# Weight splits gated on the last tiles' copies, and five register reads moved behind two transposes

## The chip, the core and the metric

The kernel runs on one core of one Trainium2 chip. Five engines work side by side: TensorE (PE in the profile, with its weight loads as PEld), VectorE (DVE), ScalarE (ACT), GpSimd (POOL) and SyncE (SP). Each has its own queue, whose instructions start in order; they wait for each other through semaphores. SP computes nothing here: it issues nearly all DMAs. The metric is the device time of one execution in microseconds (us), and of several executions the median.

## The reference

Three layers in a row: an attention with a decay bias, a dense layer with a cosine gate, and a layer of eight experts, each token going to one of them.

```python
def _attn_ref(q, k, v, s):          # 2 batches, 8 heads, 576 rows, 64 wide
    scores = scale * np.matmul(q, k.transpose(0, 1, 3, 2))
    cum = np.cumsum(np.maximum(s, 0.0), axis=-1)
    bias = -(cum[:, :, :, None] - cum[:, :, None, :])
    scores = np.where(causal, -1000000000.0, scores + np.minimum(bias, 0.0))
    attn = softmax(scores)          # written out in the reference
    return np.matmul(attn, v)

def _moe_ref(x, w_in, w_out):       # 1152 tokens, 512 -> 2048 -> 512
    h = x @ w_in
    return (h * np.cos(h)) @ w_out

def _moe2_ref(x, w_gate, w1, w2, capacity):   # 8 experts, 512 -> 1024 -> 512, capacity 288
    logits = x @ w_gate
    expert_idx = np.argmax(logits, axis=1)
    # each token is kept, in order, while its expert has had fewer than capacity tokens
    h = np.maximum(np.einsum('ecd,edf->ecf', disp, w1), 0.0)
    y = np.einsum('ecf,efd->ecd', h, w2)
    out[i] = gate_w[i] * y[expert_idx[i], pos[i]]
```

## The kernel before

The 1152 tokens are nine tiles T of 128. The attention and the first dense product (`l1`) fill the time up to about 200 us. The second dense product (`l2_mm`, line 867) makes the tiles' 512 outputs; `l2_end` copies a tile's result out of PSUM. For the last two tiles (T of 7 and 8, `T >= NDT`) it first makes a float32 copy `xq` (line 856); `route_a` turns that with four PE transposes (line 900) and copies the turned tile back to `xq` (line 902). `route_b` computes the logits and the token's place, and scatters the tile's rows into a buffer in HBM, `disp` (line 947, an indirect DMA issued by POOL), where each expert has a region of 288 rows.

After the scatter of tile 7 the first 144 rows (`HEAD`) of two experts are read from `disp`, turned by a DMA transpose into `eX` (line 1013), and computed while tile 8 is still being routed. After tile 8, `counts` finds on DVE, as integers in the tile `si`, the order of the five experts that have not been chosen yet (`si[0:5]`, line 1192) and the first row that is left of each of the two head experts (`si[8:10]`, line 1200), and in `fl` which of six sizings fits. SP reads these integers into registers, one `values_load` each, and needs them as addresses: the two first rows for the transposes of the remaining rows of the head experts, the five expert numbers for the weights and rows of the other experts.

Then the program branches on `fl`. In the arm, `experts` computes expert after expert: `e_meta` loads scale and token number of each row into `eM` (line 1020), `e_rows` a DMA transpose into `eX`, and `e_weights` streams float32 weights of 512 KB a piece into four staging buffers `ws` (lines 969 and 973). Each piece is split into two float16 halves by `split`: an ACTIVATE on ACT (line 658) and a SCALAR_TENSOR_TENSOR on DVE (line 659). `expert` multiplies with `eX` (line 1044) and the hidden tile `eH` (line 1066), turns the result (1073), scales it by `eM` (1052) and scatters it to the output (1053).

A scheduler sets the order on each engine from dependencies and from hints. A hint is given by `after`: it holds an instruction, in the schedule, behind those that a dictionary `gate` has recorded under some keys.

```python
def after(keys, fn, *args):
    with ExitStack() as es:
        for key in keys.split():
            if key in gate:
                es.enter_context(tc.issue_after(gate[key].ins))
        return fn(*args)
```

Of the kernel before, what the change touches and what calls it, by code (L numbers as in the profile page):

```python
# [14 lines left out]
AF = mybir.ActivationFunctionType  # L15
# [12 lines left out]
NK = 3  # L28
NF = 1
NH = 2  # L30
# [47 lines left out]
def kernel(ctx, tc, q, k, v, s, w_in, w_out, wg, w1, w2, out, cap, wide):  # L78
    nc = tc.nc
# [3 lines left out]
    E, _, F = w1.shape  # L83
# [12 lines left out]
    NS = -(-cap // 32) * 32  # L96
    HEAD = 144
# [47 lines left out]
    cnt = const.tile([128, 1, E], F16, name="cnt")  # L145
# [45 lines left out]
    gate = {}  # L191
# [509 lines left out]
# [6 lines that stand above are left out]
# [145 lines left out]
    def l2_end(T, xp):  # L852
        r = work.tile([128, ROW], I32, tag="row", name="row", bufs=6)
        xf = xq[:, 0:DM] if T >= NDT else None
        if T >= NDT:
            nc.scalar.activation(xf, xp, AF.Copy, scale=2.0 ** -2)
        rh = r[:, 0:DM].bitcast(F16)
        nc.scalar.activation(rh[:, 0:DM], xp, AF.Copy, scale=2.0 ** -8)
        nc.vector.scalar_tensor_tensor(rh[:, DM:2 * DM], xp, 2.0 ** -8, rh[:, 0:DM], ALU.mult, ALU.subtract)
        nc.gpsimd.tensor_copy(r[:, DM + 1:ROW], tokid[:, T:T + 1])  # L860
        rows[T] = (r, xf)
# [29 lines left out]
    def route_a(T):  # L891
        r, xf = rows[T]
        if T < NDT:
            xr = work.tile([128, 2 * KD, 128], F16, tag="xr", name="xr", bufs=2)
            nc.sync.dma_start_transpose(out=xr, in_=r[:, 0:DM].bitcast(F16))
            rows[T] = (r, xr)
        else:
            tp = bank("pt")
            for kk in range(KD):
                nc.tensor.transpose(tp[:, kk * 128:(kk + 1) * 128], xf[:, kk * 128:(kk + 1) * 128], idf)  # L900
            xt = xq[:, DM:2 * DM].rearrange("p (k t) -> p k t", k=KD)
            nc.scalar.copy(xt.rearrange("p k t -> p (k t)"), tp)
            rows[T] = (r, xt)

    def route_b(T):
# [53 lines left out]
    def e_weights(plan, lo=0, hi=None):  # L959
        n = KD + KE // 2  # L960
        items = [(e, src, i) for e, src in plan for i in range(n)][lo:hi]
        pend = []

        def ld(e, src, i):
            t = staging()
            src = src() if callable(src) else src
            if i < KD:
                s1 = w1[e, i * 128:(i + 1) * 128, :] if src is None else w1v[bass.ds(src * DM + i * 128, 128), :]
                nc.sync.dma_start(t, s1)
            else:  # L970
                j = (i - KD) * 256
                s2 = w2[e, j:j + 256, :] if src is None else w2v[bass.ds(src * F + j, 256), :]
                nc.sync.dma_start(t.rearrange("p (a d) -> p a d", a=2), s2.rearrange("(a p) d -> p a d", p=128))
            pend.append(t)

        todo = list(items)

        def fill(n):
            while todo and len(pend) < n and not (callable(todo[0][1]) and todo[0][1]() is None):
                ld(*todo.pop(0))  # L980

        fill(len(ws) - 1)
        yield
        for e, src, i in items:
            fill(len(ws))
            b_ = (win, wb[0:2], wb[2:4], wout)[e % 4]
            a = [b_[0].rearrange("p a b -> p (a b)").rearrange("p (k c f) -> p k c f", k=KD, c=2), b_[1].rearrange("p a b -> p (a b)").rearrange("p (k c f) -> p k c f", k=KE, c=2)]
            ew[e] = a
            t = pend.pop(0)
            if i < KD:  # L990
                after("ev cnt", split, a[0][:, i, 0, :], a[0][:, i, 1, :], t, 64.0)
            else:
                j = (i - KD) * 2
                after("ev cnt", split, a[1][:, j:j + 2, 0, :], a[1][:, j:j + 2, 1, :], t.rearrange("p (a d) -> p a d", a=2), 64.0)
            yield

    ex_ = {}
# [9 lines left out]
    def e_rows(e, ns, rows_):  # L1007
        i = eb["n"]
        eb["n"] += 1
        n16 = -(-ns // 16) * 16  # L1010
        xo = i % XR * 2 * KD * 224 if ns <= 224 else i % 2 * 2 * KD * n16
        X = eb["X"][:, xo:xo + 2 * KD * n16].rearrange("p (k n) -> p k n", k=2 * KD)
        nc.sync.dma_start_transpose(out=X, in_=rows_[0:n16, 0:DM].bitcast(F16))  # L1013
        ex_[e] = (X, i)
# [8 lines left out]
    def at(src, off, ns):  # L1023
        n16 = -(-ns // 16) * 16
        return disp[bass.ds(src * NS if off is None else off, n16), :]
# [63 lines left out]
    def run(*gens):  # L1089
        live = [[g, n, 0.0] for g, n in gens]  # L1090
        while live:
            live.sort(key=lambda z: z[2])
            z = live[0]
            try:
                next(z[0])
                z[2] += 1.0 / z[1]
            except StopIteration:
                live.remove(z)

    def take(gen, n):  # L1100
        for _ in range(n):
            next(gen, None)
            yield

    def seq(*gens):
        for g in gens:
            yield from g
# [36 lines left out]
    SP = (mybir.EngineType.SP,)  # L1144
# [61 lines left out]
            gate["cnt"] = V.tensor_reduce(fl, ky[:, 0:len(LIMITS)], AX.X, ALU.add)  # L1206
        return fl, si

    def registers(fl, si):
        order = [nc.values_load(si[0:1, r:r + 1], engines=SP, min_val=0, max_val=E - 1) for r in range(E - NK)]  # L1210
        first = [nc.values_load(si[0:1, E + h:E + h + 1], engines=SP, min_val=0, max_val=(E - 1) * NS + HEAD) for h in range(NH)]
        return order, first

    def experts(plan, group):
        saved = dict(ew), dict(eb), list(ws), dict(ex_)
        n = len(plan)

        def rows(e):
            src, ns, off = plan[e]
            rows_ = disp[e * NS:(e + 1) * NS, :] if src is None else at(src, off, ns)  # L1220
            if len(ex_.get(e, ())) != 2:
                e_rows(e, ns, rows_)
            e_meta(e, ns, rows_)

        depth = 2 if plan[0][1] <= 224 else 1
        for e in range(depth):
            rows(e)
        have = 0 if plan[0][0] is None else 16 + WP
        feed = e_weights([(e, plan[e][0]) for e in range(n)], have)
        gens = [expert(e, plan[e][1], group) for e in range(n)]  # L1230
        done = [0] * n
        l2s = [KD if flipped(m) else blocks(m)[0] for _, m, _ in plan]
        state = {"fed": have, "credit": -E0 * EF, "finished": 0, "l1": 0}
        next(feed)

        def pull(upto):
            while state["fed"] < min(upto, 8 * n, 8 * (state["finished"] + 4) + HALF * 4 * (state["l1"] > state["finished"])):
                next(feed)
                state["fed"] += 1

        gate.pop("ev", None)
        gate.pop("cnt", None)

        def adv(e, k):
            if e >= n:
                return
            pull(8 * (e + 1))
            while done[e] < k and next(gens[e], "end") != "end":
                done[e] += 1
                ns = plan[e][1]  # L1250
                cols = 512 * blocks(ns)[0] if not flipped(ns) else 2 * ns
                state["credit"] += EF * (12 * ns if done[e] <= KE else 12 * cols) / 2400
                pull(have + int(state["credit"]))

        la, lb = (LA, LA + LB) if depth == 2 else (0, 0)
        for e in range(n):
            if depth == 1 and e + 1 < n:
                rows(e + 1)
            adv(e, KE)
            state["l1"] = e + 1  # L1260
            adv(e + 1, la)
            if depth == 2 and e + 2 < n:
                rows(e + 2)
            adv(e, KE + l2s[e])
            adv(e + 1, lb)
            adv(e, KE + l2s[e] + 1)
            state["finished"] = e + 1
        ew.update(saved[0])
        eb.update(saved[1])
        ws[:] = saved[2]  # L1270
        ex_.clear()
        ex_.update(saved[3])
# [24 lines left out]
    with ExitStack():  # L1297
        if True:
# [35 lines left out]
            regs = counts()  # L1334
            for _ in range(KE // 2):
                next(pre)
            order, first = registers(*regs)
            for h in range(NH):
                n = max(p[h] for p in PROFILES)
                e_rows(h, n, at(P["o"][h], first[h], n))  # L1340
            run((seq(take(phase, KE - RF), take(phase1, LA), phase, phase1), 2 * (KE + KD)), (take(pre, items), W3P))
            level = nc.values_load(regs[0], min_val=0, max_val=len(LIMITS))

# [41 lines left out]
```

## Time and profile before

| | |
|---|---|
| median of three executions | 432.86 us (428.65, 432.86, 433.86) |
| the profiled execution, its own time | 430.29 us |
| its span, first to last instruction | 428.2 us |
| granted TensorE clock, mean of the span | 0.988 |
| busy: PE, DVE, ACT, POOL | 395.1, 311.8, 274.8, 149.2 us |

The span lies inside the time of the profiled execution; 2.1 us are around it. All views below are of that one execution, and their times count from the start of the span. A row of a timeline gives start, duration, engine, line, operation, tiles and, in brackets, how long the engine had been idle before it and what ended that.

### The profile page before, as it was taken

To read this page: it belongs to the slowest core of one execution; us is meant where nothing else is said; L and a number is where in the kernel's file an instruction comes from. 1 tells how busy PE (TensorE), PEld (TensorE's weight loads), DVE (VectorE), ACT (ScalarE), POOL (GpSimd) and SP (SyncE) were. 2 spreads that over 40 slices of the span, in tenths; PEclk is the share of its full clock that TensorE was granted. 3 is DMA by queue.
4 is the path that set the end of the run, shared out by engine and by line. 5 is a ranking of instruction groups with operands and counts; after the bars stand their busy time and mean duration, and the time that the engine had idled before them with its cause. 6 is when DMAs were issued, how large, how long until landed. Compare 5 with 4: busy or idle time off the path is not lost.

```text
span 428.2 us, 10640 instructions
## 1 busy us (share of the span) xinstructions
PE 395.1 (92%) x3928; PEld 281.6 (66%) x3928; DVE 311.8 (73%) x768; ACT 274.8 (64%) x630; POOL 149.2 (35%) x261
## 2 busy tenths in 40 slices
PE   2799999999999999999999999797998999999783
PEld 2588888886666666654444454354997999987552
DVE  7769999749999599989885664672842477877670
ACT  6679989986878677775234532533734477777560
POOL 7668887563554445455000032010011011122100
PEclk9989999999999999999999999899999999999998
DMA  7979795203369932323667456947759298998851
GB/s 166 210 173 190 165 203 151 72 2 100 98 188 328 369 124 92 88 70 98 183 204 230 116 128 206 280 110 222 252 148 216 61 314 264 308 330 265 264 209 30
DMA packets 90003, 77.38 MB, mean 181 GB/s; under 512 B 62768, under 2 KB 70960, under 8 KB 89942
## 3 DMA queue, kind: packets, MB, share of 16 engines
q1 hardware_dynamic: 86934, 71.62, 59.5%
q0 software_dynamic: 1952, 4.73, 3.2%
q8 instruction: 33, 0.54, 0.5%
q10 hardware_dynamic: 1056, 0.26, 0.3%
q14 instruction: 28, 0.23, 0.2%
HBM read 57.66 MB, written 12.28 MB: 163 GB/s over the span
## 4 chain that ended last, share of the span: by engine, by line
PE 32%; DMA 9%; DVE 7%; issue 5%; ACT 4%; SPq 2%; POOL 1%; POOLq 0%; ACTq 0%; DVEq 0%
DMA ws<-in_moe_w_dram 8%; PE ps_mm L867 7%; PE ps_sm L867 5%; PE ps_pt L1044 3%; PE ps_s L1066 3%; PE ps_mm L1044 2%; PE ps_s L867 2%; PE ps_pt L867 2%; PE ps_s L1044 2%; PE ps_pt L1066 2%; PE ps_mm L1066 2%; DVE gall L659 1%; ACT gall L658 1%; DVE y L818 1%; SPq L1013 1%
## 5 line engine op out<-in xcount | busy, mean ns | idle before, releaser
L812 PEld LDWEIGHTS <-win 128*128 128x128 f16 x576 | 56.3, 98 | 37.0
L867 PEld LDWEIGHTS <-gall 128*128 128x128 f16 x432 | 41.3, 98 | 49.3 <-issue 2.5
L867 PE MATMUL ps_mm<-wout,gall 128*128 128x512 f16 x240 | 57.9, 387 | 0.3 <-DVE n__2954 L826 0.3
L659 DVE SCALAR_TENSOR_TENSOR gall<-ws,gall 128x1024 f16<-128x1024 f32 x32 | 38.8, 1221 | 23.2 <-ACT gall L658 22.1
L1053 POOL DMA_INDIRECT out_dram<-gall,eM x15 | 18.8, 1252 | 98.4 <-ACT gall L1052 77.4
L658 ACT ACTIVATE gall<-ws 128x1024 f16<-128x1024 f32 x32 | 33.7, 1056 | 26.8 <-DMA ws<-in_moe_w_dram 26.8
L658 ACT ACTIVATE wout<-ws 128x512 f16<-128x512 f32 (+1 forms) x32 | 27.3, 860 | 23.7 <-DVE ws L681 18.5
L241 ACT ACTIVATE z<-z,st 128x256 f32<-128x256 f32 (+4 forms) x72 | 41.9, 586 | 0.7 <-DVE st L241 0.7
L947 POOL DMA_INDIRECT disp<-row,rsli x9 | 9.2, 1017 | 94.0 <-ACT rm L928 48.5
L241 DVE CUSTOM_DVE_ANT_0 z<-ps_s,zm 128x512 f32<-128x512 f32 (+3 forms) x72 | 34.5, 511 | 10.0 <-PE ps_s L244 8.8
L659 DVE SCALAR_TENSOR_TENSOR wout<-ws,wout 128x512 f16<-128x512 f32 (+1 forms) x32 | 30.4, 955 | 8.2 <-ACT wout L658 8.0
L812 PE MATMUL ps_s<-xT,win 128*128 128x384 f16 x192 | 34.2, 326 | 0.0
L812 PE MATMUL ps_pt<-xT,win 128*128 128x384 f16 x192 | 33.8, 326 | 0.0
L812 PE MATMUL ps_mm<-xT,win 128*128 128x384 f16 x192 | 33.8, 326 | 0.0
L247 PE MATMUL ps_pt<-idf,z 128*128 128x128 f32 x192 | 30.2, 282 | 1.3 <-DVE p L241 1.3
L1044 PEld LDWEIGHTS <-gall 128*128 128x128 f16 x480 | 27.0, 97 | 3.7 <-issue 1.9
L825 ACT ACTIVATE y<-y,quarter 128x384 f32<-128x384 f32 x48 | 29.2, 609 | 0.1
L241 ACT COPY p<-ps_pt 128x512 f32<-128x512 f32 (+2 forms) x48 | 25.2, 525 | 5.9 <-PE ps_pt L247 5.5
L659 DVE SCALAR_TENSOR_TENSOR win<-ws,win 128x1024 f16<-128x1024 f32 x16 | 19.4, 1225 | 11.7 <-ACT win L658 11.7
L247 PEld LDWEIGHTS ps_pt<-idf,z 128*128 128x128 f32 x192 | 23.1, 144 | 6.3 <-issue 1.5
L244 PE MATMUL ps_s<-kT,qT 128*128 128x384 f16 (+7 forms) x128 | 23.9, 307 | 1.1 <-DMA kT<-bt 0.6
L658 ACT ACTIVATE win<-ws 128x1024 f16<-128x1024 f32 x16 | 16.8, 1055 | 10.9 <-DMA ws<-in_moe_w_dram 10.9
(495 smaller groups left out, 891.9 us busy)
## 6 DMA issues: line engine op xcount, KB each, us to landing
ws<-in_moe_w_dram SPq DMA_DIRECT2D x64, 512.0 KB
ws<-in_moe_w_in_dram SPq DMA_DIRECT2D x16, 512.0 KB
ws<-in_moe_w_out_dram SPq DMA_DIRECT2D x16, 512.0 KB
disp<-zc SPq DMA_DIRECT2D x18, 257.0 KB
out_dram<-zc SPq DMA_DIRECT2D x9, 256.0 KB
qf<-in_q_dram SPq DMA_DIRECT2D x16, 128.0 KB
vf<-in_v_dram SPq DMA_DIRECT2D x16, 128.0 KB
kf<-in_k_dram SPq DMA_DIRECT2D x14, 128.0 KB
```

Of the source, the lines that this page charges most:

```text
L241: return pin(f(*a, **kw))
L244: return pin(nc.tensor.matmul(out_, **kw))
L247: return pin(nc.tensor.transpose(out_, in_, id_))
L658: nc.scalar.activation(hi, src, AF.Copy, scale=sc)
L659: (eng or nc.vector).scalar_tensor_tensor(lo, src, sc, hi, ALU.mult, ALU.subtract)
L812: nc.tensor.matmul(hp[:, 0:CH], lhsT=win[a][:, kk, fs], rhs=xT[:, x_, kk, xs], start=(n == 0), stop=(n == 3 * KD - 1))
L825: nc.scalar.activation(y, y, AF.Sin, scale=TWO_PI, bias=quarter)
L867: gate["pe"] = nc.tensor.matmul(xp, lhsT=G[c][:, a, f, ts], rhs=wout[w_][:, f, :], start=(f == 0 and n == 0), stop=(f == KF - 1 and n == 2))
L947: sc = nc.gpsimd.indirect_dma_start(out=disp, out_offset=bass.IndirectOffsetOnAxis(ap=sli.bitcast(U32), axis=0), in_=r, in_offset=None, bo ...
L1044: gate["pe"] = nc.tensor.matmul(hp[:, 0:ns], lhsT=a1[:, kk, a, fs], rhs=X[:, x_ * KD + kk, 0:ns], start=(n == 0), stop=(n == 3 * KD - 1))
L1053: sc = nc.gpsimd.indirect_dma_start(out=out, out_offset=bass.IndirectOffsetOnAxis(ap=M[:, b, 1:2].bitcast(U32), axis=0), in_=y, in_offset= ...
L1066: nc.tensor.matmul(yp[:, 0:ns], lhsT=a2[:, f, w_, d * 128:(d + 1) * 128], rhs=Hh[:, a, f, :], start=(n == 0), stop=(n == 3 * KE - 1))
```

## The change

Two edits. First, the copies of the last two tiles to `xq` are recorded in `gate["xq"]`, and the splits of the experts' weights are hinted behind them, as they were behind `ev` and `cnt` already. Second, the seven register reads on SP are parted: the two first rows are read, then the two transposes of the remaining rows are issued, then the five expert numbers are read.

```diff
@@ l2_end
         if T >= NDT:
-            nc.scalar.activation(xf, xp, AF.Copy, scale=2.0 ** -2)
+            gate["xq"] = nc.scalar.activation(xf, xp, AF.Copy, scale=2.0 ** -2)
@@ route_a
-            nc.scalar.copy(xt.rearrange("p k t -> p (k t)"), tp)
+            gate["xq"] = nc.scalar.copy(xt.rearrange("p k t -> p (k t)"), tp)
@@ e_weights (and the same in its other arm)
-                after("ev cnt", split, a[0][:, i, 0, :], a[0][:, i, 1, :], t, 64.0)
+                after("ev cnt xq", split, a[0][:, i, 0, :], a[0][:, i, 1, :], t, 64.0)
@@
-    def registers(fl, si):
-        order = [nc.values_load(si[0:1, r:r + 1], engines=SP, min_val=0, max_val=E - 1) for r in range(E - NK)]
-        first = [nc.values_load(si[0:1, E + h:E + h + 1], engines=SP, min_val=0, max_val=(E - 1) * NS + HEAD) for h in range(NH)]
-        return order, first
+    def registers(si):
+        return [nc.values_load(si[0:1, E + h:E + h + 1], engines=SP, min_val=0, max_val=(E - 1) * NS + HEAD) for h in range(NH)]
+
+    def others(si):
+        return [nc.values_load(si[0:1, r:r + 1], engines=SP, min_val=0, max_val=E - 1) for r in range(E - NK)]
@@ experts
-        gate.pop("ev", None)
-        gate.pop("cnt", None)
+        for key in ("ev", "cnt", "xq"):
+            gate.pop(key, None)
@@
-            order, first = registers(*regs)
+            first = registers(regs[1])
             for h in range(NH):
                 n = max(p[h] for p in PROFILES)
                 e_rows(h, n, at(P["o"][h], first[h], n))
+            order = others(regs[1])
```

On SP, after the last weights of the head experts, the order before had all seven reads of `si` ahead of the two transposes into `eX`. TENSOR_LOAD is a read, and the ISA rows behind it are register arithmetic; the semaphore in brackets is what the instruction waits for, DMASW0 being that of the scatter of tile 8. Four more pairs of reads like the first stand ahead of this piece.

```order
L1210 TENSOR_LOAD si
L1210 ISA x2
L1211 TENSOR_LOAD si [waits DVE_49]
L1211 ISA x2
L1211 TENSOR_LOAD si
L1211 ISA x2
L1013 ISA
L1013 DMA_TRANSPOSE eX<-disp 128x8x80 [waits DMASW0_49]
L1013 ISA
L1013 DMA_TRANSPOSE eX<-disp 128x8x80
L1342 TENSOR_LOAD fl [waits DVE_49]
```

In the changed kernel the same place on SP begins with the two reads of the first rows (now line 1210), and line 1213 is that of the other experts' numbers.

```order
L1210 TENSOR_LOAD si [waits DVE_49]
L1210 ISA x2
L1210 TENSOR_LOAD si
L1210 ISA x2
L1013 ISA
L1013 DMA_TRANSPOSE eX<-disp 128x8x80 [waits DMASW0_49]
L1013 ISA
L1013 DMA_TRANSPOSE eX<-disp 128x8x80
L1213 TENSOR_LOAD si
L1213 ISA x2
```

Five reads have moved from ahead of the transposes to behind them; four more pairs like the last follow, then the read of `fl`, the branch and the arm's DMAs, which stand as before. The transposes keep their wait.

On ACT, these are the rows around the copies of tile 8 (`xq`, lines 856 and 902) and the weight splits (line 658) in the changed kernel.

```order
L658 ACTIVATE gall<-ws_90 128x1024 [waits DMAHW7_49]
L856 ACTIVATE xq<-ps_mm 128x512 [waits PE_49]
L858 ACTIVATE row<-ps_mm 128x512 [waits DMAHW6_49,DMASW2_49,Pool_49]
L658 ACTIVATE gall<-ws_91 128x1024 [waits DMAHW0_49]
L902 COPY xq<-ps_pt 128x512 [waits PE_49]
```

Nothing has moved here: the kernel before has the same five rows with the same waits, and on ACT, DVE, PE and POOL all other rows stand in the same order too, apart from their line numbers.

## Rows read from the trace of the kernel before

**Rows 1.** The page, busy time of each engine, share of the span, instructions.
```profile
PE 395.1 (92%) x3928; PEld 281.6 (66%) x3928; DVE 311.8 (73%) x768; ACT 274.8 (64%) x630; POOL 149.2 (35%) x261
```

**Rows 2.** The chain that ended last: start us, duration us, what.
```profile
291.45 3.62 DMA ws<-in_moe_w_dram
...
326.68 1.24 issue
...
365.72 5.36 DMA ws<-in_moe_w_dram
...
390.54 7.19 DMA ws<-in_moe_w_dram
```

**Rows 3.** Timeline at tile 8's copies, ACT and PE.
```profile
295.09 1.06 ACT L658 ACTIVATE gall<-ws 128x1024 f16<-128x1024 f32 x1 [7.80 <-DMA ws<-in_moe_w_dram]
296.05 0.58 ACT L856 ACTIVATE xq<-ps_mm 128x512 f32<-128x512 f32 x1
...
296.68 0.65 PE L900 MATMUL ps_pt<-idf,xq 128*128 128x128 f32 x4 [2.95 <-ACT xq L856]
```

**Rows 4.** SP's register reads by line: duration ns min/median/max, first and last start us.
```profile
L1210 SPq TENSOR_LOAD <-si x5: 172/272/488, 304.9 to 307.2; - x5
...
L1211 SPq TENSOR_LOAD <-si x2: 275/276/276, 308.0 to 308.9; - x2
...
L1211 SPq SEQ_ASSERT  x2: 18/18/18, 308.5 to 309.4; - x2
```

**Rows 5.** Timeline of the scatter of tile 8 and of DVE's first rows.
```profile
305.44 0.97 POOL L947 DMA_INDIRECT disp<-row,rsli  x1 [11.89 <-DVE ky L1198]
...
305.79 0.14 DVE L1200 TENSOR_TENSOR si<-ky,prow 1x2 int32<-1x2 f32 x1
```

**Rows 6.** SP's waits, 304 to 312 us: who waited for what, us, times, longest.
```profile
SPq L1013 <- DMA disp<-row,rsli: 1.1, 1, 1.1
```

**Rows 7.** Timeline of SP's DMA issues from the transposes of the remaining rows on.
```profile
310.64 2.77 SPq L1013 DMA_TRANSPOSE eX<-disp  x2
314.41 1.24 SPq L1020 DMA_DIRECT2D eM<-disp  x2
316.06 1.84 SPq L969 DMA_DIRECT2D ws<-in_moe_w_dram  x3
318.17 3.06 SPq L1013 DMA_TRANSPOSE eX<-disp  x1
...
322.80 2.64 SPq L1013 DMA_TRANSPOSE eX<-disp  x1
325.65 0.41 SPq L1020 DMA_DIRECT2D eM<-disp  x1
329.61 6.60 SPq L1013 DMA_TRANSPOSE eX<-disp  x2
340.71 4.62 SPq L973 DMA_DIRECT2D ws<-in_moe_w_dram  x3
```

**Rows 8.** Timeline of the first instructions on PE and ACT that use these DMAs.
```profile
325.00 0.53 PE L1044 MATMUL ps_pt<-eX,win 128*128 128x64 f16 x12 [0.72 <-ACT gall L1052]
...
327.92 0.25 PE L1044 MATMUL ps_pt<-eX,win 128*128 128x64 f16 x3 [1.24 <-issue]
...
335.23 1.07 PE L1044 MATMUL ps_pt<-eX,gall 128*128 128x176 f16 x12
...
345.37 0.93 PE L1044 MATMUL ps_mm<-eX,wout 128*128 128x160 f16 x11
...
330.32 1.05 ACT L658 ACTIVATE wout<-ws 128x1024 f16<-128x1024 f32 x1
...
335.43 0.68 ACT L1052 ACTIVATE gall<-ps_s,eM 64x512 f32<-64x512 f32 x1 [0.24 <-PE ps_s L1073]
338.37 1.05 ACT L658 ACTIVATE wout<-ws 128x1024 f16<-128x1024 f32 x1
```

**Rows 9.** Windows: us, PE, PEld, DVE, ACT, POOL busy, PEclk, DMA share, GB/s.
```profile
325.00:330.00 5.00, 3.73 (x120) 3.58 (x121) 1.58 (x8) 2.01 (x10) 1.84 (x2) 1.00 0.88 256
330.00:335.00 5.00, 5.00 (x177) 4.91 (x174) 2.46 (x9) 2.98 (x13) 0.00 (x0) 1.00 0.34 69
```

More of the change, by code (lines that the diff above doesn't have):

```diff
@@ L990, in e_weights @@
             if i < KD:
-                after("ev cnt", split, a[0][:, i, 0, :], a[0][:, i, 1, :], t, 64.0)
+                after("ev cnt xq", split, a[0][:, i, 0, :], a[0][:, i, 1, :], t, 64.0)
             else:
                 j = (i - KD) * 2
-                after("ev cnt", split, a[1][:, j:j + 2, 0, :], a[1][:, j:j + 2, 1, :], t.rearrange("p (a d) -> p a d", a=2), 64.0)
+                after("ev cnt xq", split, a[1][:, j:j + 2, 0, :], a[1][:, j:j + 2, 1, :], t.rearrange("p (a d) -> p a d", a=2), 64.0)
             yield
```

## The prediction

> **What bounds the kernel now.** I read the page first, then the chain that ended last, then the timelines around the two edits. PE is busy for 92% of the span [rows 1], but that share is an average over stages; what counts here is 290 to 345 us, where tile 8 is routed, the registers are read and the arm begins. In that stretch the chain goes through a weight transfer at 291.45, then over PE with short pieces of ACT and DVE; the only long piece that is not work is a pause of PE of 1.24 us at 326.68, put down to its own issue. From 365.72 on the chain comes back to weight transfers, again and again, with pieces of 3.62 to 7.19 us from an issue to the split that waited [rows 2]. So two things could pay: to get PE past tile 8 sooner, or to bring weights earlier in the arm. SP's register reads are in no piece of this chain.
>
> At tile 8 there is a real loss. ACT sat 7.80 us in front of a split whose weights had not landed; the copy to `xq`, which needs no weights, stood behind that split and began at 296.05, and PE was idle for 2.95 us until it came [rows 3]. That is the stall which a hint "splits behind the copies" could remove.
>
> **First edit: the hint on `xq`.** The order of the changed program, shown ahead of this text, is the same on ACT as before: the split that waits for its weights still stands in front of the copy of tile 8, and a second split still stands between that copy and the one of line 902. The reason can be seen in the code: a split is held behind the copy that was recorded last when the split was written down, and these splits are written before tile 8's copies exist, so they are held behind those of tile 7, where they stood already. No instruction is added, none moves, no wait is added: the cost is 0.0 us, and the 2.95 us stay. No other engine has a row that moved because of it either.
>
> **Second edit: the reads on SP.** Only SP's queue changes; SP also gains no instruction and loses none, five reads change places with two transposes. Step by step:
>
> *What a read costs.* Five reads ran from 304.9 to 308.0, so 3.1 us, or 0.62 us each with the register arithmetic behind them; the two of the first rows ran from 308.0 to 309.4, 1.4 us [rows 4].
>
> *When the transposes start.* The two first rows are written by DVE at 305.79 + 0.14 = 305.93 [rows 5]. SP now waits for that instead of for the earlier half of `si`, reads twice, and stands ready at 305.93 + 1.4 = 307.3, where before it was ready at about 309.5. But the transposes read what the scatter of tile 8 writes. SP, once ready, still waited 1.1 us for that scatter [rows 6], and the transposes went out at 310.64 [rows 7], which is 5.2 us after the scatter was issued at 305.44 [rows 5]. Nothing in this edit touches the scatter. So the transposes go out at 310.64 again; only SP's wait grows, from 1.1 to 3.3 us. The gain at this place is 0.0 us. Had the scatter landed at once, the transposes would be 2.2 us earlier than SP was ready before, and even that would be worth nothing: the first multiplication with remaining rows starts at 325.00 [rows 8], 11.6 us after the second transpose was issued (310.64 + 2.77 = 313.41) [rows 7], and its wait of 0.72 us is put down to ACT.
>
> *What the moved reads push back.* The five reads now stand between 313.41 and the read of `fl`, so everything behind them on SP is up to 3.1 us later: the branch, the loads of `eM` (314.41 to 317.5), three weight pieces (316.06 to 319.2), the transpose for the third expert (318.17 to 321.3), a fourth weight piece, the transpose for the fourth expert (322.80 to 325.9) and one more load of `eM` (325.65 to 328.75, done by 329.2). The next instruction, a transpose, went out at 329.61 because its part of `eX` was still being read by PE: SP had nothing to do from 326.06 to 329.61, 3.55 us [rows 7]. The 3.1 us fit into that with 0.4 us over. From 329.61 on SP is where it was, and the waits up to the next weight piece at 340.71 are still there in full. The other engines read `fl` for themselves, so their branches do not wait for SP's.
>
> *Who uses what comes late.* The first split in the arm ran at 330.32, without idle time before it, and the second at 338.37 [rows 8]. The three pieces are issued by 316.06 + 1.84 + 3.1 = 321.0; with the longest transfer of the chain, 7.19 us [rows 2], they have landed by 328.2, 2.1 us before the first split. The third expert's `eX` is issued by 318.17 + 3.06 + 3.1 = 324.3 and first used at 335.23; the fourth's by 328.5 and first used at 345.37; the first use of an `eM` that is loaded here is at 335.43 [rows 8], 17 us after its issue. Every cover is longer than 3.1 us, the thinnest being the first split's. If that cover were gone, the price would be the full 3.1 us; a gain I exclude, since no chain piece waits for SP here. Between 0 and 3.1 us I take 0.0, by the row of the split with no wait before it.
>
> The Trainium skill (DMA: Bandwidth & Descriptors, Anatomy of one DMA) puts a DMA issued by GpSimd at about 2.0 us plus its bytes over 436 GB/s. For the 263 KB of a tile's rows that makes an estimate of 2.6 us from that page, a landing at 308.0, and by it the reads would have held the transposes back before; they would now start 1.5 us sooner, and what follows the five reads would be 1.6 us late instead of 3.1. The trace speaks against it with its 5.2 us from issue to the transposes; and by either figure the total stays, since the covers above are longer than both.
>
> *Sum:* 0.0 (hint) + 0.0 (transposes) + 0.0 (reads, covered) = no change against the profiled execution's own 430.29 us. The four executions shown (428.65, 430.29, 432.86, 433.86) have their middle at 431.6; the profiled one lies 1.3 us under it. I forecast **431.6 us**.
>
> **The rivals.** *The late weights are felt (slower).* The mechanism is SP's queue: 3.1 us more in front of the arm's first weight pieces. For it speaks that the chain after 365 us is made of weight transfers, so that a stream which is shifted as a whole would shift the end. It decides once the first split at 330.32 waits, which it does if a piece takes more than 330.32 - 321.0 = 9.3 us to land, or once SP's 3.55 us of spare time are less than the reads take. Against it: 7.19 us is the longest transfer of the chain, and the next weight piece went out at 340.71, 4.5 us after SP had issued the transposes ahead of it (329.61 + 6.60 = 336.21) [rows 7], so that stream is not paced by SP. Price 3.1 us, so 434.7 us.
>
> *The transfers are crowded into the branch (slower).* The DMA engines were busy for 0.88 of 325 to 330 and for 0.34 of 330 to 335 [rows 9]; the same transfers 3.1 us later move most of that load into the second stretch, where PE runs its smallest matmuls, 177 in 5 us without a gap. PE paused once in the loaded stretch, for 1.24 us at 326.68 with nothing to wait for that the profile shows [rows 2, 8]; a second such pause makes 431.6 + 1.24 = 432.8 us. Against it: PE's pause came soon after its branch and needs no DMA load to explain it. The Trainium skill (Runtime: NRT & Kernel Launch, Instruction fetch mechanics) says that a taken branch out of the fetched window stalls until a DMA has fetched the target page; by that rule a busier DMA stretch right behind the branch would lengthen the pause, but no row here ties the pause to a fetch.
>
> *The hint does what it says (faster).* If the splits came behind tile 8's copies after all, PE would get its 2.95 us back: 428.7 us. The order of ACT speaks against it; the rows that would have to move have not moved.
>
> **How the numbers follow.** No change 0.78; crowding 0.10; late weights 0.08; hint 0.02; 0.02 for something else. All of these lie inside 2% of 431.6, which is 8.6 us and about what a measurement of this kernel can tell from no change, so the chances are made by the scatter of the executions and by what I have not thought of: faster 0.015, within 2% 0.965, slower 0.02. The range takes the four executions and, since four are few, a quarter of their spread of 5.2 us below the lowest: 427.4 us. Above, the highest plus the price of crowding, which also covers the late weights on a middle execution: 433.86 + 1.24 = 435.1 us.
>
> **What the changed kernel's profile would show.** The split and the copy of tile 8 in the old order, with PE's idle time of about 3 us before line 900 still there. SP's wait for the scatter at the transposes at about 3.3 us instead of 1.1, the transposes at 5.2 us after the scatter as before. Five reads of line 1213 over about 3.1 us behind them, the `eM` loads and the three weight pieces about 3.1 us later against PE's work, and SP's spare time before the transpose at 329.61 down to about 0.4 us. The first split of the arm without a DMA wait. I am wrong if that split waits for its weights, if PE's pauses behind the branch add up to over 2.5 us, or if the scatter lands so much earlier or later in the new order that the transposes start more than 2 us away from it.

## The result and the profile after

The changed kernel took 433.63 us (median of 22 executions, 429.81 to 437.84), the kernel before 431.27 us (median of 22, 428.04 to 434.26). The ratio is 1.0056, 95% interval 1.003 to 1.0081: the change costs about 2.4 us. The ratios, here and below, leave out executions that lie over 1.5% above the fastest of the same kernel. The loss is well within 2%, but it is not the 0.0 of the sum.

The profiled execution of the changed kernel took 435.38 us, with a span of 433.2 us, 5.0 us longer than the one before. Of these, 1.78 us lie ahead of PE's branch into the arm, and 1.37 of them are there at the first matmul of line 867 (191.96 us instead of 190.59), where no instruction has moved: that part is a difference between two executions and not the change.

First the places that the prediction spoke of. The page's busy row:

```profile
PE 398.7 (92%) x3928; PEld 284.2 (66%) x3928; DVE 311.8 (72%) x768; ACT 274.9 (63%) x630; POOL 149.7 (35%) x261
```

The counts are those of [rows 1]; PE is busy 3.6 us longer with the same 3928 matmuls, which alone says little: a kernel below that lost nothing, delay10_now, has 398.3 us. Tile 8, timeline of the kernel after (compare [rows 3]):

```profile
296.71 1.06 ACT L658 ACTIVATE gall<-ws 128x1024 f16<-128x1024 f32 x1 [7.66 <-DMA ws<-in_moe_w_dram]
297.67 0.58 ACT L856 ACTIVATE xq<-ps_mm 128x512 f32<-128x512 f32 x1
...
298.30 0.66 PE L900 MATMUL ps_pt<-idf,xq 128*128 128x128 f32 x4 [2.81 <-ACT xq L856]
```

The split still goes first and PE still waits for the copy behind it. Next SP, kernel after: the five reads (duration ns min/median/max, first and last start), SP's wait for the scatter, and the DMA issues that answer to [rows 7].

```profile
L1213 SPq TENSOR_LOAD <-si x5: 269/279/732, 315.2 to 317.9; - x5
```

```profile
SPq L1013 <- DMA disp<-row,rsli: 3.5, 1, 3.5
```

```profile
312.52 2.60 SPq L1013 DMA_TRANSPOSE eX<-disp  x2
319.85 1.25 SPq L1020 DMA_DIRECT2D eM<-disp  x2
321.43 2.30 SPq L969 DMA_DIRECT2D ws<-in_moe_w_dram  x3
323.99 1.81 SPq L1013 DMA_TRANSPOSE eX<-disp  x1
326.08 0.49 SPq L1020 DMA_DIRECT2D eM<-disp  x1
326.91 0.35 SPq L969 DMA_DIRECT2D ws<-in_moe_w_dram  x1
327.47 2.27 SPq L1013 DMA_TRANSPOSE eX<-disp  x1
329.95 0.41 SPq L1020 DMA_DIRECT2D eM<-disp  x1
331.09 10.07 SPq L1013 DMA_TRANSPOSE eX<-disp  x2
```

SP went nearly as worked out: the transposes 5.2 us after the scatter (issued at 307.27), as before. PE left its branch at 326.65 here and at 324.87 before. Counted from that branch, the three weight pieces go out 5.2 us ahead of it instead of 8.8 us, and the transpose that closes SP's spare time 4.4 us behind it instead of 4.7 us. SP had caught up. PE had not: its chain, kernel after.

```profile
328.28 0.44 issue
...
328.99 0.49 issue
...
331.96 0.30 PE ps_s L1044 x12
...
332.97 0.58 PE ps_mm L1066 x20
333.55 2.53 issue
336.08 0.28 PE ps_mm L1066 x4
...
337.97 0.48 PE ps_mm L1044 x12
```

PE stands still for 0.44 + 0.49 + 2.53 = 3.46 us, where it stood for 1.24 us before [rows 2, 8], and no semaphore is waited for ("issue"). Behind the long pause the matmuls are slow: twelve of 48 columns take 0.48 us, and 0.30 us ahead of it. The 401st matmul behind PE's branch starts 15.52 us after the branch in the kernel before and 19.18 us in the kernel after: 3.66 us lost, 2.22 of them in pauses and the other 1.4 us in slower matmuls. From that matmul to the end of the span it is 87.8 and 87.4 us, so nothing more is lost further on. The windows of the kernel after (columns as in [rows 9]) show both:

```profile
325.00:330.00 5.00, 3.30 (x74) 2.60 (x73) 0.41 (x3) 2.21 (x7) 1.87 (x2) 1.00 1.09 308
330.00:335.00 5.00, 3.55 (x129) 3.46 (x126) 3.13 (x12) 2.79 (x11) 0.00 (x0) 1.00 1.34 223
335.00:340.00 5.00, 3.92 (x102) 3.88 (x102) 0.62 (x3) 1.34 (x7) 0.00 (x0) 0.74 0.20 44
```

The DMA share of 330 to 335 is 1.34 instead of 0.34 (0.46 in the same stretch counted from the branch, 328.22 to 333.22; a share adds up the time of all packets, so it can pass 1), and the granted clock behind it is 0.74 (a stretch at both of its levels, 2.4 and 1.2 GHz), where it was 1.00. The first two splits of the arm, kernel after, wait for no DMA:

```profile
331.80 1.05 ACT L658 ACTIVATE wout<-ws 128x1024 f16<-128x1024 f32 x1
...
343.81 1.05 ACT L658 ACTIVATE wout<-ws 128x1024 f16<-128x1024 f32 x1
```

So the loss lies on PE, behind its branch, in pauses for which the profile shows no wait for data. Instructions come by DMA too. The page of the kernel after, part 3, has two queues for them (packets, MB, share):

```profile
q8 instruction: 33, 0.54, 0.5%
...
q14 instruction: 28, 0.23, 0.2%
```

33 packets of 16 KB for 2 x 3928 matmuls and weight loads is one packet for some 240 instructions, so I take q8 to be PE's. I counted this queue in three stretches, first of the kernel before, 329 to 331 us (4.1 to 6.1 us after the branch):

```profile
q1 hardware_dynamic: 27, 0.01, 4.0%
q8 instruction: 1, 0.02, 3.8%
```

then of the kernel after, 326.7 to 333.5 us, and after it 333.5 to 334.9 us:

```profile
q1 hardware_dynamic: 3228, 1.62, 102.1%
q0 software_dynamic: 109, 0.23, 11.8%
```

```profile
q1 hardware_dynamic: 628, 0.13, 173.3%
q0 software_dynamic: 17, 0.04, 9.9%
q8 instruction: 1, 0.02, 4.8%
```

Before, a packet of instructions passes from 329.08 to 330.28 us, in a quiet moment. After, none passes for 6.8 us; the next lasts from 333.62 to 334.69 us, when SP's queue moves less (0.13 MB in 1.4 us, after 1.62 MB in 6.8 us), and 1.39 us after its end PE goes on.

### The profile page after: what moved, and what is told of

The parts are those of the page before. It is cut to its first block, busy times and chain, and to the rows that moved or that the text cites. A ratio compares the mean times of both kernels' runs of the same rounds, so it can differ in the third digit from the quotient of the medians.

```text
span 433.2 us, 10640 instructions
## 1 busy us (share of the span) xinstructions
PE 398.7 (92%) x3928; PEld 284.2 (66%) x3928; DVE 311.8 (72%) x768; ACT 274.9 (63%) x630; POOL 149.7 (35%) x261
## 5 line engine op out<-in xcount | busy, mean ns | idle before, releaser
L867 PEld LDWEIGHTS <-gall 128*128 128x128 f16 x432 | 41.3, 98 | 49.9 <-issue 3.2
L1044 PEld LDWEIGHTS <-gall 128*128 128x128 f16 x480 | 28.0, 100 | 3.0 <-issue 1.1
```

The costliest lines, as they stand in the source:

```text
L867: gate["pe"] = nc.tensor.matmul(xp, lhsT=G[c][:, a, f, ts], rhs=wout[w_][:, f, :], start=(f == 0 and n == 0), stop=(f == KF - 1 and n == 2))
L1044: gate["pe"] = nc.tensor.matmul(hp[:, 0:ns], lhsT=a1[:, kk, a, fs], rhs=X[:, x_ * KD + kk, 0:ns], start=(n == 0), stop=(n == 3 * KD - 1))
```

## The experiments

Two theories. **F** (fetch): SP's delayed transfers are in flight when PE's next instructions have to be fetched; the fetch is held up and PE runs dry. **W** (weights): the arm's stream of weights is late as a whole, and something downstream feels it. A rival of both is that the reads hurt at their new place for another reason. "Pauses" below are PE's idle times over 0.4 us between matmuls in the 40 us behind its branch; the profile names no releaser for them but PE's own issue, except for those with a star, which it puts down to an instruction of DVE. "First packet" is the start and end of the first packet of q8 behind that branch, the last column the start of the 401st matmul, both in us behind the branch. These three columns come from the one profiled execution of each kernel, the ratios from the timed ones.

| kernel | ratio to before, 95% interval | pauses, us | first packet, us | 401st matmul, us |
|---|---|---|---|---|
| before | | 1.24 | 4.21 to 5.42 | 15.52 |
| after | 1.0056, 1.003 to 1.0081 | 0.44 + 0.49 + 2.53 | 6.97 to 8.04 | 19.18 |
| after_again | one execution, 432.56 us (before 431.75) | 0.49 + 0.51 + 2.44 | 6.93 to 7.93 | 19.15 |
| hint_only | 1.0005, 0.9979 to 1.0032 | none | 2.76 to 3.65 | 13.77 |
| delay5 | 1.0061, 1.0018 to 1.0103 | 1.07 | 4.25 to 5.21 | 15.00 |
| delay10 | 1.0115, 1.0084 to 1.0146 | 2.23 + 0.77* | 4.63 to 6.37 | 17.09 |
| before_nox | 1.0056, 1.0013 to 1.0098 | none | 2.22 to 3.48 | 13.77 |
| after_nox | 1.0064, 1.0025 to 1.0104 | none | 2.47 to 3.47 | 13.78 |
| before_nox2 | 0.9975, 0.9934 to 1.0015 | none | 2.35 to 3.73 | 13.87 |
| delay10_nox | 1.0039, 1.0006 to 1.0071 | 1.99 | 5.29 to 6.17 | 15.92 |
| before_now | 0.9997, 0.9966 to 1.0029 | 0.54* | 2.41 to 3.58 | 14.47 |
| delay10_now | 0.9961, 0.9925 to 0.9996 | 0.60* | 2.82 to 4.14 | 14.56 |
| delay10_dummy | 1.0114, 1.0063 to 1.0164 | 0.64* + 2.50 + 0.77* | 5.92 to 7.25 | 18.16 |
| before_crowd | 1.0100, 1.0066 to 1.0133 | 0.48 + 2.14 | 3.61 to 4.50 | 18.22 |

**hint_only: the first edit alone.** The reads stay where they were.

```diff
...
-                after("ev cnt", split, a[0][:, i, 0, :], a[0][:, i, 1, :], t, 64.0)
+                after("ev cnt xq", split, a[0][:, i, 0, :], a[0][:, i, 1, :], t, 64.0)
...
```

> The kernel before with the order of the splits behind tile 8's xq asked for and the five reads left where they were: the instructions of all engines stand as before. Both theories: 0.998 to 1.002, a control for what a measurement of this kind gives on the same program.

1.0005: the hint does nothing, and all of the loss belongs to the second edit. As this is the program of before, its profile also shows that the 1.24 us of [rows 2] are not there in every execution: here PE did not pause at all. Up to the 401st matmul the profile of the changed kernel is 5.4 us behind this one and 3.66 us behind that of before, so one pair of profiles does not give the price of the change; the ratio does.

**delay5: the delay without the new order.** The kernel before with five more reads, their result unused but for the order of the experts, behind the transposes.

```diff
             for h in range(NH):
                 n = max(p[h] for p in PROFILES)
                 e_rows(h, n, at(P["o"][h], first[h], n))
+            order = [nc.values_load(regs[1][0:1, r:r + 1], engines=SP, min_val=0, max_val=E - 1) for r in range(E - NK)]
```

> The order of the kernel before, with five register reads of the same words added behind the two transposes: SP's DMAs of the arm are 3.1 us later, but no read leaves its old place. Two theories of the slowdown. F (fetch): PE runs out of instructions behind its branch, because the DMAs that SP issues in the arm, now later, are in flight just when PE's next instructions are fetched. W (weights): the stream of weights of the arm is later as a whole, and the end with it. Both expect the changed kernel's ratio, 1.003 to 1.008. F expects in the trace PE pauses with no releaser that add up to over 2.5 us between PE's branch and the third expert's first matmul, and no DMA wait before the first split of the arm; W expects that split, or one of the next three, to wait for its DMA. If the ratio is 1.000, it was neither, but the reads of the first rows in their new place.

1.0061, the loss of the change. What costs is that SP's DMAs in the arm go out later, not where the reads have gone. None of the arm's first four splits waits for its weights, against W. But the pauses of over 2.5 us that F expected are not in the trace either: the profiled execution, with 429.71 us the third fastest of twelve, has one of 1.07 us. The pauses differ from one execution to the next, as between before and hint_only.

**delay10: twice the delay.** The changed kernel with the five reads done twice.

```diff
+            others(regs[1])
             order = others(regs[1])
```

> The changed kernel with the five reads behind the transposes done twice, so SP's arm is 6.2 us later than before. W expects the loss to double at least: ratio 1.011 to 1.016. F expects no proportion: the loss depends on which transfers are in flight at the two or three moments when PE fetches, 1.000 to 1.009.

1.0115, twice the loss for twice the delay. That is above what F allowed for and inside the range of W: a miss for F's number. In the trace none of the arm's first four splits waits for a transfer, and the pauses are 3.0 us. That is less than the 3.46 us of the changed kernel, in the fastest of the twelve executions, so no trace shows the doubled loss.

**before_nox, after_nox: without three transposes.** The transposes of the third to fifth expert in the arm are left out; these experts multiply old rows or zeros, so their outputs are not computed. POOL clears `eX` first.

```diff
...
+        nc.gpsimd.memset(eb["X"][:, 0:3 * 2 * KD * 224], 0.0)
...
-        nc.sync.dma_start_transpose(out=X, in_=rows_[0:n16, 0:DM].bitcast(F16))
+        if load:
+            nc.sync.dma_start_transpose(out=X, in_=rows_[0:n16, 0:DM].bitcast(F16))
...
```

> The kernel before without the DMA transposes of the third to fifth expert's rows in the arm (those experts multiply old or zero rows, so their outputs are not the reference's). F expects PE's 1.24 us pause behind the branch to shrink or go: ratio 0.994 to 0.999. W expects 1.000.

> The changed kernel without the same three transposes. F, if the transposes are what delays the fetch, expects no loss against before_nox: a ratio within 0.002 of that one's, and no pause of PE of over 1.3 us in the arm's first 15 us. W expects the full loss against before_nox, 0.004 to 0.007.

1.0056 and 1.0064: against each other the pair differs by 0.0008, but the half-widths combine to about 0.006, too wide to tell no loss from that of the change. What speaks is the traces: neither has a pause. That both are slower than before, which neither theory had allowed for, fits the clearing of `eX`, 4.58 us on POOL at 204 us: counted from the first matmul of line 867, the scatter of tile 7 went out 3.4 us later in after_nox than in after (105.70 instead of 102.31 us). With other clears, below, that loss is gone.

**before_nox2, delay10_nox: the same with small clears on DVE, and the doubled delay.**

```diff
...
+        for i_, lo_ in enumerate((144, 144, 80)):
+            nc.vector.memset(eb["X"][:, 2 * KD * (224 * i_ + lo_):2 * KD * 224 * (i_ + 1)], 0.0)
...
```

> The kernel before without the DMA transposes of the third to fifth expert's rows in the arm, like before_nox, but the unwritten parts of eX are zeroed by three small DVE writes in place of one on POOL, which had cost some 3 us ahead of the branch. It is the base for delay10_nox. F expects no PE pause behind the branch and a ratio of 0.995 to 1.001 with the cost of the zeroing in it; W expects the zeroing's cost alone, 1.000 to 1.004.

> delay10 without the same three transposes: SP's arm is 6.2 us later than in before_nox2, and nothing else differs. delay10 lost 1.15%. F, if it is these transposes that delay PE's fetch, expects the ratio of before_nox2 within 0.003 and no pause. W expects 0.009 to 0.014 more than before_nox2, since the weights are late by as much as in delay10.

0.9975 and 1.0039, a difference of 0.0064 (half-widths combined, about 0.005): with 6.2 us of delay the loss is back without these transposes, with a pause of 1.99 us. Both expectations missed: F's (within 0.003 and no pause, if these transposes were the crowd) and W's (0.009 to 0.014). So the transposes are at most a part of the crowd and not its core.

**before_now, delay10_now: without the first four weight transfers.** The arm's first four pieces are not loaded; their splits work on what stood in the staging buffers.

```diff
...
+            left[0] -= 1
+            if left[0] >= 0:
+                pend.append(t)
+                return
...
```

> The kernel before without the arm's first four weight transfers (the splits take what lies in the staging buffers, so outputs are not the reference's). It is the base for delay10_now. F: the pause may shrink, since 2 MB fewer are in flight; 0.993 to 1.000. W: 1.000.

> delay10 without the same four weight transfers. W expects no loss against before_now, within 0.002, since no split can wait for a late weight there. F expects that a loss stays as far as the transposes alone delay the fetch, 0.004 to 0.012 more than before_now, with PE pauses in the trace.

0.9997 and 0.9961: without these transfers the same 6.2 us of delay on SP, with all reads and transposes in place, cost nothing. The loss needs the four weight transfers. F had expected 0.004 to 0.012 more than before_now here, from the transposes alone: a miss. That the weight transfers make the crowd fits W as well as F, since leaving them out takes away the crowd and the dependence together; the next two part them.

**delay10_dummy: the crowd without the dependence.** As delay10_now, but the four transfers are issued, into spare DRAM that nobody reads. The four pieces never reach the staging buffers.

```diff
...
+            put = t if left[0] < 0 else dw[left[0]]
...
-                nc.sync.dma_start(t, s1)
+                nc.sync.dma_start(put, s1)
...
```

> The changed kernel with the five reads done twice (about 6.2 us later on SyncE), and the arm's first four weight transfers read the same 512 KB each but write them to spare DRAM that nothing reads, so the first four splits work on old data (wrong weights for those pieces) and can wait for no transfer. The crowd of transfers is kept and the dependence is taken away. W (weights come late as a whole): as without the transfers, 0.996 to 1.002, TensorE's pauses behind its branch at most 0.7 us. F (the transfers hold up TensorE's fetch of its instructions): as with the 6.2 us delay, 1.006 to 1.015, pauses of 2 us or more, the first large packet of the instruction queue later than 4.5 us after the branch.

1.0114, against 0.9961 for delay10_now, whose instructions on ACT, DVE and PE stand in the same order. Nothing can wait for these transfers, and the loss is there in full. W falls. The row of PE's timeline, delay10_dummy:

```profile
336.07 0.28 PE L1070 MATMUL ps_mm<-eH,win 128*128 128x64 f16 x4 [2.50 <-issue]
```

**before_crowd: the crowd without the delay.** The kernel before, its delays untouched, and four spare transfers of 512 KB in SP's idle time.

```diff
...
+                if e == 1:
+                    with tc.issue_after(gate["eM"].ins):
+                        for i in range(4):
+                            nc.sync.dma_start(dw[i], w1[0, i * 128:(i + 1) * 128, :])
```

> The kernel before with every read, transpose and weight transfer of the arm where it was, and four extra transfers of 512 KB from DRAM to spare DRAM that nothing reads, issued in SyncE's idle time before 329.61 us. Nothing that is used comes late up to then. F: the extra crowd meets TensorE's fetch behind its branch, pauses of 2 us or more instead of 1.24 us, ratio 1.003 to 1.010. W: nothing is late, so 0.997 to 1.003 and the pause stays near 1.24 us. Computes the same result.

1.0100: nothing that is used before the pauses was late, and the kernel is 1% slower. One transpose, for a later expert, goes out at 343.89 us, behind both pauses, and no instruction waits for it. SP's row, then PE's timeline, then two windows, all of before_crowd:

```profile
327.09 3.23 SPq L1268 DMA_DIRECT2D dw<-in_moe_w_dram  x4
```

```profile
331.53 0.28 PE L1067 MATMUL ps_mm<-eH,win 128*128 128x64 f16 x4 [0.48 <-issue]
...
338.82 0.39 PE L1045 MATMUL ps_s<-eX,gall 128*128 128x176 f16 x3 [2.14 <-issue]
```

```profile
335.00:340.00 5.00, 2.86 (x36) 2.71 (x34) 0.68 (x2) 1.21 (x3) 0.93 (x1) 0.96 1.08 100
340.00:345.00 5.00, 5.00 (x115) 5.00 (x114) 1.82 (x3) 2.38 (x7) 0.00 (x0) 0.70 0.18 60
```

Here too the clock falls behind the long pause. The spare transfers are not quite the original ones: they also write to DRAM, and in larger pieces, and in this kernel they come on top of the load instead of moving it. So the two runs show what kind of cause it is, not its exact price.

**after_again: a second profile of the changed kernel.** Nothing is edited.

> The changed kernel unaltered, a second profile of it. F: TensorE stops behind its branch again, pauses of 1.5 us or more in sum, with the first large packet of the instruction queue later than 4.5 us after the branch, and no split of the arm's first four waits for a transfer. W: no pause over 1.3 us in sum, and a split or a matmul that waits for a transfer of weights.

As F expected: three pauses, each within 0.1 us of those in the first profile, with the long one in front of the same matmul, and the 401st matmul at 19.15 us instead of 19.18:

```profile
335.04 0.28 PE L1066 MATMUL ps_mm<-eH,win 128*128 128x64 f16 x4 [2.44 <-issue]
```

**Where PE stops.** Over all these traces there are ten pauses that end later than 6 us behind the branch, in seven profiles, and every one stands in front of one of two instructions: the 189th matmul behind the branch (after, after_again, delay5, delay10, delay10_nox, delay10_dummy, before_crowd) or the 317th (delay10, delay10_dummy, before_crowd). These are 128 matmuls apart, 256 instructions with their weight loads. Each of them ended 1.3 to 1.6 us after a packet of the instruction queue had ended.

Where PE did not stop, these matmuls came later behind their packet: the 189th at least 1.77 us behind the end of the first packet, in the other seven profiles, the 317th at least 1.84 us behind that of the second. So in all fourteen profiles the end of the packet tells whether PE stops, and the kernel before, with its 1.77 us, had little to spare. A fetch in blocks would give both, the two fixed places and the fixed distance from a packet; a wait for data would not follow the packets.

The Trainium skill (Runtime: NRT & Kernel Launch, Instruction fetch mechanics) has instructions fetched in blocks of 16 KiB, 256 instructions each; the distance of 128 matmuls agrees with it. It calls the cost of a block's boundary mostly hidden; here it was up to 2.53 us.

Two kinds of pause need a word. Rows of PE's timeline, first of delay10, then of before_now:

```profile
337.02 0.31 PE L1044 MATMUL ps_s<-eX,gall 128*128 128x176 f16 x2 [0.77 <-DVE eH L1047]
```

```profile
330.00 0.51 PE L1049 MATMUL ps_pt<-eX,win 128*128 128x64 f16 x12 [0.54 <-DVE eH L1052]
```

The 0.77 us in front of the 317th matmul (delay10, delay10_dummy) are put down to DVE, but the changed kernel has the same order on PE and DVE, and there this matmul starts at 342.49 us, ahead of that DVE instruction at 343.04; I count them with the fetch. The 0.54, 0.60 and 0.64 us in front of the 73rd (before_now, delay10_now, delay10_dummy) are waits for DVE: they end 0.05 us after DVE has read `ps_pt`, and DVE had been held for 1.2 us by a split that waited for no weights. The pauses of 0.4 to 1.24 us in the first 3.1 us behind the branch in before, after and after_again have no packet right ahead of them, and what makes them stays open.

## Why the prediction was wrong, point by point

- **The hint, 0.0 us: right.** Tile 8's rows are unchanged, and hint_only gives 1.0005.
- **The transposes, 0.0 us: right.** 5.2 us after the scatter again, SP's wait 3.5 us where 3.3 were expected.
- **The reads push back SP's DMAs by 3.1 us: right but short.** The five reads took 315.17 to 318.86, 3.7 us, with one load of 0.73 us among them; SP caught up in its spare time all the same.
- **"Who uses what comes late": the step that failed.** It put the late transfers at 0.0 us, and they cost 2.4. Its covers were right: no consumer of a late transfer waited, and the first split was in time. But the list held only the instructions that use the transfers. By these runs the DMA engines have another user, PE's instruction fetch, whose first packet behind the branch ended at 5.42 us in the kernel before and at 8.04 in the kernel after. Before, SP's 3.55 us of spare time [rows 7] left it a gap, with a DMA share of 0.34 from 330 to 335 [rows 9]. I had counted it as slack; the change filled it.
- **The rival "crowded into the branch" was the right mechanism, with too small a chance and price.** It had 0.10 and 1.24 us, the price of one more pause like the one seen. Measured by the ratio the change costs 2.4 us; in the profile it is 2.22 us of pauses and 1.4 us of slower matmuls behind them. What I held against it, that a pause soon after a branch needs no DMA load to explain it, may hold for that pause, whose cause stays open; it is another kind of pause that grew. The mark "PE's pauses behind the branch add up to over 2.5 us" was met, with 3.46 us. The rule of the Trainium skill (Runtime: NRT & Kernel Launch, Instruction fetch mechanics) that the prediction cites has PE stall at a taken branch; in these runs the stalls that a busier stretch lengthened came not at the branch itself but at the blocks that follow it.
- **The rival "late weights" was wrong** in its mechanism (delay10_dummy), though its 3.1 us are near the size, which is luck.
- **The forecast of 431.6 us** lies 2.0 us under the measured median of 433.63 us. That this is inside the range is no merit of the sum: the range was made of the scatter of the executions, and the sum had no change where there is a loss.

What is shown: the loss comes with SP's delay (delay5), needs the weight transfers (delay10_now), does not need that anybody waits for them (delay10_dummy), and comes without any delay when other transfers are put there (before_crowd). That the resource in between is PE's fetch is argued from the fixed places and the packets; no run changed the fetch by itself. No version tried here is a better kernel: those without the crowd leave work out, and of them only delay10_now (0.9961) lies clear of the kernel before.

## What to carry to other kernels

When an edit delays DMAs, list not only who uses their data but who else needs the DMA engines at the new time; a stretch in which a queue is idle may be the gap in which an engine's instructions come in; here that mattered up to 15 us behind a branch. A pause of PE without a releaser ("issue") in front of the same instruction in several profiles, with a packet of the instruction queue ending shortly before it, is the sign, and it can have a releaser by chance. To part "late" from "crowded", send the same transfers to a place that nobody reads.

## What was not expected of the hardware

- For 6.8 us behind PE's branch no packet of instructions passed, while 1.62 + 0.23 = 1.85 MB of other queues did, though SP's DMAs and PE's instructions are in different queues.
- After pauses of PE of 2.53, 2.44 and 2.14 us the mean granted clock of a 5 us window fell to 0.74, 0.66 and 0.70 (after, after_again, before_crowd), a mixture of the two levels; after pauses of 2.23 and 2.50 us it stayed at 1.00 (delay10, delay10_dummy). What decides it is open.
- One and the same program (before, hint_only) paused for 1.24 us behind its branch in one profile and not at all in another.
